# A Block whose closing barrier leaves out the drain of GpSimd

## The chip, the cores and the metric

The kernel runs on one core of a Trainium2 chip. The metric is the device time of one execution in microseconds (us).

Three stretches of the end of an execution are used throughout, all read from the trace:

- **A**: from the landing of the last output DMA to the end of the Block's last semaphore instruction. That instruction also ends the profile's span, except in one experiment, which is marked.
- **B**: from there to the last semaphore event of the record. It lies outside the span. In the trace of the kernel before it has nine counts of semaphore 2 between 829.68 and 830.27 us, then events of 196 semaphores, then nine counts again between 831.05 and 831.41 us. No recorded instruction of the program names semaphore 2. This document and the recorded texts call each group of nine counts a barrier of the runtime; the name is the author's reading.
- **G**: the pause between the two semaphore instructions with which GpSimd closes the Block (the first collects the arrivals of the other engines, the second lets them go).

A + B is the whole serial tail after the last byte of output has landed.

## The reference

A transformer block: layernorm with a modulation, linear attention, layernorm with a modulation, and a gated feed-forward part.

```python
def reference(A_x, A_wqkv, A_wo, B_x, B_w_gate, B_w_up, B_w_down, c, w_mod):
    ...                                   # A_x: 1 x 2048 x 1024, bf16
    mod = (_silu(c) @ w_mod).reshape(c.shape[0], 6, 1, -1)
    ...
    h = _layernorm(x, axis=-1) * (1 + ca) + sa
    x = x + ga * _A_ref(h, A_wqkv, A_wo)              # linear attention, 32 heads
    h = _layernorm(x, axis=-1) * (1 + cb) + sb
    x = x + gb * _B_ref(h, B_w_gate, B_w_up, B_w_down)  # silu(h @ gate) * (h @ up) @ down
    return x
```

The change does not touch the arithmetic.

## The kernel before

The kernel records a list of operations for each engine, works out the semaphore waits between them, and emits one program per engine into a Block. When the Block closes, all engines meet in a barrier. The parts that matter here are the Block, GpSimd's own work (57 small operations, no DMA), and the end of SyncE's program, which waits for every output DMA.

```python
    with ExitStack() as es:
        block = es.enter_context(nc.Block())
        ...
        P.pool("memset", ap=IDENT[:], constant=1.0)            # GpSimd's program begins
        P.pool("affine_select", out=IDENT[:], in_=IDENT[:], ...)
        P.pool("memset", ap=NEGHALF[:], constant=-0.5)
        ...
        def th2_mod():                                         # and ends with the fourth of these
            for dt in range(NDT):
                P.pool("tensor_scalar", out=H2T[:, dt, :], in0=H2T[:, dt, :], scalar1=MODCOL[:, 2, dt:dt + 1],
                       scalar2=MODCOL[:, 3, dt:dt + 1], op0=ALU.mult, op1=ALU.add)
        ...
                        out_ops.append(P.dma("out", ov[:, st, nh * 512 + c0:nh * 512 + c1], xs))   # from SyncE
        P.wait_for("sp", out_ops)
        ...
        engines = {"pe": block.tensor, "act": block.scalar, "dve": block.vector, "pool": block.gpsimd,
                   "sp": block.sync}
        P.emit(sems, engines)
```

As built, the Block of the kernel before closes in this way. TensorE, VectorE, ScalarE and SyncE each execute a DRAIN that also counts up a semaphore (96), and then wait for another one (97). GpSimd executes a plain DRAIN, waits until semaphore 96 stands at four, and raises semaphore 97 by four.

## Time and profile before

| | |
|---|---|
| time, median of the first 3 runs | 831.32 us (831.20 to 831.43) |
| span of the profiled run | 829.4 us |
| TensorE (PE) busy | 824.0 us, 99% |
| GpSimd (POOL) busy | 39.8 us, 5% |
| A, B, G | 0.771, 1.970, 0.414 us |

The first lines of the page of the kernel before give the span and each engine's busy time.

```profile
span 829.4 us, 10017 instructions
...
PE 824.0 (99%) x4083; PEld 378.4 (46%) x4083; DVE 312.0 (38%) x665; ACT 197.6 (24%) x336; POOL 39.8 (5%) x57
...
```

The chain of waits of the kernel before, in order of time (start us, us, what):

```profile
...
1.71 4.21 DMA xres<-in_A_x_dram
...
8.76 818.08 PE ps L176 x4069
826.83 0.02 issue
826.86 0.29 DVE xres L176
```

Between 8.76 and 826.84 us the chain is TensorE alone. As long as another engine does not keep TensorE waiting, it can only cost time before or after that stretch.

The next view has the instructions of the Block's own line (286) in the kernel before: engine, operation, count, then shortest, median and longest duration in ns, then the start of the first and of the last in us. The letter q marks the engine's sequencer.

```profile
...
L286 POOLq EVENT_SEMAPHORE  x2: 17/17/17, 828.9 to 829.3; - x2
L286 POOLq DRAIN  x1: 6939/6939/6939, 642.8 to 642.8; - x1
...
L286 SPq COMPARE_BRANCH  x1: 41/41/41, 828.7 to 828.7; - x1
L286 SPq DRAIN  x1: 13/13/13, 828.9 to 828.9; - x1
L286 SPq EVENT_SEMAPHORE  x1: 17/17/17, 829.4 to 829.4; - x1
...
```

GpSimd's DRAIN is the longest record of the group (6939 ns), but it starts at 642.8 us, 186 us before the barrier. A duration in such a list says nothing about cost until the start has been read. The two semaphore instructions of GpSimd start 0.4 us apart, at 828.9 and 829.3. The DMA queues of the kernel before (packets, MB, share):

```profile
...
q1 hardware_dynamic: 199184, 118.65, 52.7%
q8 instruction: 32, 0.52, 0.3%
q14 instruction: 13, 0.11, 0.0%
q10 hardware_dynamic: 16, 0.00, 0.0%
...
```

There is no queue of a software kind: GpSimd issues nothing.

The same tail with exact times, listed from the trace's instruction records (us from the start of the span; duration in ns):

```
last matmul ends            826.817
SyncE   last output issued  827.174
        last landing        828.668
SyncE   branch              828.684   41
SyncE   DRAIN (arrives)     828.865   13
GpSimd  semaphore 96 >= 4   828.903   17
GpSimd  semaphore 97 += 4   829.334   17     <- 0.414 us after the one before it ended
others  semaphore 97 >= 1   829.376 (first start) to 829.439 (last end)
        last event          831.409
```

In this trace the record of GpSimd's first semaphore instruction starts only when its semaphore is satisfied: the fourth arrival is counted at 828.879 us, and the record starts 0.024 us later, though GpSimd's instruction before it, the DRAIN, had ended at 649.773 us. The second one, which raises semaphore 97, has no semaphore to wait for at all, so the 0.41 us between them are not a wait for an engine that these records show.

### The profile page before, as it was taken

To read this page: it belongs to the slowest core of one execution; us is meant where nothing else is said; L and a number is where in the kernel's file an instruction comes from. 1 tells how busy PE (TensorE), PEld (TensorE's weight loads), DVE (VectorE), ACT (ScalarE), POOL (GpSimd) and SP (SyncE) were. 2 spreads that over 40 slices of the span, in tenths; PEclk is the share of its full clock that TensorE was granted. 3 is DMA by queue.
4 is the path that set the end of the run, shared out by engine and by line. 5 is a ranking of instruction groups with operands and counts; after the bars stand their busy time and mean duration, and the time that the engine had idled before them with its cause. 6 is when DMAs were issued, how large, how long until landed. Compare 5 with 4: busy or idle time off the path is not lost.

```text
span 829.4 us, 10017 instructions
## 1 busy us (share of the span) xinstructions
PE 824.0 (99%) x4083; PEld 378.4 (46%) x4083; DVE 312.0 (38%) x665; ACT 197.6 (24%) x336; POOL 39.8 (5%) x57
## 2 busy tenths in 40 slices
PE   8999999999999999999999999999999999999998
PEld 4544444454444444444444444444444444444444
DVE  5797986756955521121221111122111111221111
ACT  4757641323242111011111101111110111111011
POOL 1010000000130000030000003000000300000000
PEclk9999999999999999999999999999999999999999
DMA  9969655928397996700455570045557004553000
GB/s 320 288 151 229 149 159 172 202 102 304 60 258 225 259 267 174 192 25 14 128 150 155 150 188 28 15 126 153 153 153 187 26 18 125 154 151 86 0 26 26
DMA packets 199245, 119.28 MB, mean 144 GB/s; under 512 B 57880, under 2 KB 182944, under 8 KB 199200
## 3 DMA queue, kind: packets, MB, share of 16 engines
q1 hardware_dynamic: 199184, 118.65, 52.7%
q8 instruction: 32, 0.52, 0.3%
q14 instruction: 13, 0.11, 0.0%
q10 hardware_dynamic: 16, 0.00, 0.0%
HBM read 100.67 MB, written 4.33 MB: 127 GB/s over the span
## 4 chain that ended last, share of the span: by engine, by line
PE 99%; DMA 1%; DVE 0%; ACT 0%; SPq 0%; issue 0%
PE ps L176 99%; DMA xres<-in_A_x_dram 1%; DVE stats L176 0%; ACT xres L176 0%; SPq L176 0%; DVE xres L176 0%; DVE mv L176 0%; DVE nmr L176 0%
## 5 line engine op out<-in xcount | busy, mean ns | idle before, releaser
L176 PE MATMUL ps<-h2t,gug 128*128 128x512 bf16 x896 | 211.7, 379 | 0.0
L176 PE MATMUL ps<-h2t,guu 128*128 128x512 bf16 x896 | 211.7, 379 | 0.0
L176 DVE TENSOR_TENSOR at<-sg,ps 128x512 bf16<-128x512 bf16 x112 | 77.1, 688 | 282.7 <-PE ps L176 281.1
L176 ACT ACTIVATE sg<-ps 128x512 bf16<-128x512 f32 x112 | 66.9, 597 | 309.7 <-PE ps L176 309.7
L176 PEld LDWEIGHTS ps<-h2t,guu 128*128 128x128 bf16 x896 | 87.5, 98 | 105.8
L176 PEld LDWEIGHTS ps<-h2t,gug 128*128 128x128 bf16 x896 | 87.4, 98 | 105.7
L176 PE MATMUL ps<-wd_a,at 128*128 128x512 bf16 (+1 forms) x512 | 112.4, 378 | 0.0
L176 PE MATMUL ps<-ht,wqk 128*128 128x512 bf16 x512 | 111.7, 379 | 0.0
L176 PE MATMUL ps<-wd_b,at 128*128 128x512 bf16 (+1 forms) x384 | 85.0, 378 | 0.0
L176 PEld LDWEIGHTS ps<-wd_a,at 128*128 128x128 bf16 x512 | 50.0, 98 | 59.8
L176 DVE TENSOR_TENSOR ut<-att,gb_b 128x512 bf16<-128x512 bf16 (+1 forms) x32 | 13.8, 430 | 167.5 <-ACT att L176 167.5
L176 PEld LDWEIGHTS ps<-ht,wqk 128*128 128x128 bf16 x512 | 49.4, 98 | 58.8
L176 ACT ACTIVATE att<-ps 128x512 bf16<-128x512 f32 (+1 forms) x32 | 17.4, 591 | 182.1 <-PE ps L176 182.1
L176 PEld LDWEIGHTS ps<-wd_b,at 128*128 128x128 bf16 x384 | 37.5, 98 | 44.7
L176 PE MATMUL ps<-pk,xres 128*128 128x512 bf16 x256 | 56.5, 379 | 0.0
L176 PE MATMUL ps<-mw,pqt 128*128 128x512 bf16 x256 | 56.3, 379 | 0.0
L176 POOL TENSOR_SCALAR h2t<-h2t,modcol 128x512 bf16<-128x512 bf16 x32 | 26.4, 841 | 383.0 <-DMA h2t<-xn 383.0
L176 ACT ACTIVATE e<-ps 128x512 bf16<-128x512 f32 x56 | 33.1, 603 | 31.7 <-PE ps L176 20.5
L176 PEld LDWEIGHTS ps<-mw,pqt 128*128 128x128 bf16 x256 | 24.8, 98 | 30.3 <-DVE xres L176 0.4
L176 PEld LDWEIGHTS ps<-pk,xres 128*128 128x128 bf16 x256 | 24.8, 98 | 30.0 <-issue 0.4
L176 ACT ACTIVATE junk<-xres 128x1024 bf16<-128x1024 bf16 x24 | 25.4, 1058 | 35.1 <-DVE xres L176 34.9
L176 DVE SCALAR_TENSOR_TENSOR xres<-ps,xres 128x512 bf16<-128x512 f32 x32 | 21.4, 689 | 12.3 <-PE ps L176 11.7
(107 smaller groups left out, 346.0 us busy)
## 6 DMA issues: line engine op xcount, KB each, us to landing
gug<-in_B_w_gate_dram SPq DMA_DIRECT2D x56, 512.0 KB, 3.9
guu<-in_B_w_up_dram SPq DMA_DIRECT2D x56, 512.0 KB, 5.2
xres<-in_A_x_dram SPq DMA_DIRECT2D x20, 256.0 KB, 7.8
rb<-recip_den SPq DMA_DIRECT2D x8, 512.0 KB, 11.5
stgx<-in_w_mod_dram SPq DMA_DIRECT2D x2, 2048.0 KB, 7.8
wd_a<-in_B_w_down_dram SPq DMA_DIRECT2D x4, 1024.0 KB, 7.8
out_dram<-xres SPq DMA_DIRECT2D x31, 128.0 KB, 1.7
xres<-in_A_x_dram SPq DMA_DIRECT2D x3, 1024.0 KB, 14.0
```

Source lines behind the costliest of these rows:

```text
L176: return getattr(e, method)(**kw)
```

## The change

The intent is to end the Block without the drain of GpSimd, as GpSimd has no DMA in this kernel. The other engines are still to drain, and all engines to meet in a barrier of semaphores alone.

```diff
     with ExitStack() as es:
-        block = es.enter_context(nc.Block())
+        block = es.enter_context(nc.Block(no_gpsimd_drain=True))
```

As built, this removes GpSimd's DRAIN and gives each of the other four engines one semaphore instruction more: their DRAIN no longer counts up semaphore 96, a separate instruction behind it does.

## The prediction

> What bounds the kernel now. TensorE does: the page's first part gives PE 824.0 us busy of a span of 829.4 us (99%), and the chain of waits is PE from 8.76 us to 826.84 us almost without a break. The granted clock is 1.000. Only the first 8.8 us and the tail after the last matmul are not TensorE.
>
> The tail, read from the instructions of the Block's own line (line 286) and from the semaphore events: the last matmul ends at 826.84, VectorE adds until 827.15, SyncE issues the last output DMA at 827.17, it has landed at 828.67, and only then SyncE leaves its program (828.68) and runs its DRAIN (828.87, 13 ns). GpSimd sees the fourth arrival at 828.90, and releases everybody at 829.33; the others see it at 829.38 to 829.45. So the whole barrier after the last landing takes about 0.75 us, 0.09% of the time.
>
> What the change removes. One DRAIN of GpSimd. In the trace this DRAIN starts at 642.83 and lasts 6.94 us, ending at 649.77; it is long because it stands behind eight operations on GpSimd, the last of which ends at 649.71. It is over 178 us before the last output lands, so it is not on the critical path. Nor is there anything in a ring for it to wait for: no instruction of GpSimd issues a DMA. [...] all data packets (199,184 + 16) are of kind hardware_dynamic, issued by SyncE and ScalarE.
>
> What it adds. By the description of the flag the other four engines still drain, and then pass a barrier of semaphores alone. That may add one semaphore instruction on each engine; these last 17 to 51 ns each here. On SyncE, the last to arrive, this would be on the critical path: I estimate +0.03 to +0.1 us from those durations and from the 24 ns between SyncE's arrival and GpSimd's start.
>
> What it may move. Between GpSimd's two semaphore instructions lie 0.41 us at the end, but 0.06 us in the same pair at the program's start (0.583 to 0.600, then 0.661). I can't tell from this trace why. If the new barrier is built of other instructions, some of this 0.41 us may go. That is the most there is to gain: 0.41/831, 0.05%.
>
> Sum: between -0.4 and +0.15 us. The three runs before spread by 0.23 us, so the change should hardly be seen. Nothing in the engine programs themselves changes.
>
> Predicted time: 831.2 us, range 830.6 to 831.8. Chances: faster by over 2%: 0.004; within 2%: 0.992; slower by over 2%: 0.004.
>
> What would show each step right: in the profile after, GpSimd's DRAIN of the Block's line is gone (or no longer a plain DRAIN), its last multiplications still end near 650 us, PE's busy time stays within 1 us of 824.0, the last output DMA still lands about 1.5 us after issue, and the stretch from that landing to the last semaphore instruction is 0.3 to 0.9 us. Wrong: a changed PE busy time, a lower clock, or a tail longer than 1 us.
>
> What would make it wrong: a barrier of semaphores whose hops are serial through all five engines and dear; a runtime epilogue outside the span (the time exceeds the span by 1.8 us) which depends on that drain, so that its cost shows up there; or chips that differ by more than the 0.03% that the three runs show.

## The result

The kernel after took 831.42 us (median of 6 runs, 830.86 to 831.73), the kernel before 831.22 us (median of 6, 830.89 to 831.43). The ratio of fast runs is 1.0002, with a 95% interval of 0.9989 to 1.0015: the same. Ratios in this document are the mean time of one kernel's fast runs over that of the other's of the same rounds, so not quite the ratio of the medians quoted.

The page of the kernel after begins:

```profile
span 828.6 us, 10020 instructions
...
PE 823.5 (99%) x4083; PEld 379.1 (46%) x4083; DVE 312.6 (38%) x665; ACT 197.7 (24%) x336; POOL 39.9 (5%) x57
...
```

Its chain of waits:

```profile
...
1.69 3.68 DMA xres<-in_A_x_dram
...
8.21 818.07 PE ps L176 x4069
...
826.31 0.29 DVE xres L176
```

The span is 0.8 us shorter than before, and the change did not cause most of that. The matmul stretch is as long as before (818.07 against 818.08 us) but starts 0.55 us earlier, because the first input load on the chain took 3.68 us in place of 4.21. The change has not touched that load, and it varies from run to run: an experiment below has 4.47 us. A single pair of spans would have misled here.

The instructions of the Block's line in the kernel after:

```profile
...
L286 DVEq EVENT_SEMAPHORE  x2: 21/21/21, 826.7 to 828.6; - x2
L286 SPq EVENT_SEMAPHORE  x2: 17/17/17, 828.4 to 828.6; - x2
L286 POOLq EVENT_SEMAPHORE  x2: 17/17/17, 828.4 to 828.5; - x2
...
L286 SPq COMPARE_BRANCH  x1: 41/41/41, 828.1 to 828.1; - x1
L286 SPq DRAIN  x1: 7/7/7, 828.3 to 828.3; - x1
...
```

GpSimd's DRAIN is gone, SyncE has two semaphore instructions in place of one, and the two of GpSimd now start 0.1 us apart. With exact times, from the trace:

```
                        before     after
last landing           828.668   828.133
A                        0.771     0.496
G                        0.414     0.065
B                        1.970     2.414
A + B                    2.741     2.910
```

So the pause of 0.41 us did go out of the Block's barrier, and A became 0.275 us shorter. But B, outside the span, became 0.444 us longer. The runtime's own barrier shows where: each arrival counts up one semaphore (2), and between the second and the third count there lie 0.267 us before and 0.688 us after. In the runtime's last barrier before the program, and in the second of the two behind it, 0.038 us lie there, in both kernels. The sum moved by +0.17 us.

The times say the same about B without any trace of it: the device time less the span is 2.16 to 2.26 us in the six runs after, and 1.74 to 1.84 us in nine later runs of the kernel before. The two ranges are far apart, although the times themselves overlap.

### The profile page after: what moved, and what is told of

Same layout as the page of the kernel before. It is cut to its first block, busy times and chain, and to the rows that moved or that the text cites. A ratio compares the mean times of both kernels' runs of the same rounds, so it can differ in the third digit from the quotient of the medians.

```text
span 828.6 us, 10020 instructions
## 1 busy us (share of the span) xinstructions
PE 823.5 (99%) x4083; PEld 379.1 (46%) x4083; DVE 312.6 (38%) x665; ACT 197.7 (24%) x336; POOL 39.9 (5%) x57
## 4 chain that ended last, share of the span: by engine, by line
PE 99%; DMA 0%; DVE 0%; ACT 0%; SPq 0%; issue 0%
PE ps L176 99%; DMA xres<-in_A_x_dram 0%; DVE stats L176 0%; ACT xres L176 0%; SPq L176 0%; DVE xres L176 0%; DVE mv L176 0%; DVE nmr L176 0%
```

## The experiments

Two theories are tested.

- **Theory S (slot)**: the 0.41 us belongs to a fixed place in GpSimd's instruction stream. Removing the DRAIN moved every later instruction one place forward, so the pause fell on the next one, behind the program, where B lies. The cause supposed, that the next block of instructions is asked for at this place, is an estimate from a packet of 8,192 bytes on an instruction queue that starts at 830.06 us in the kernel before; no record shows it.
- **Theory D (drain)**: the pause is an after-effect of GpSimd's DRAIN, and the longer B is the runtime making up for a drain that was left out.

The results of the runs about the place of the pause, from their profiles (the four runs with late work or with a DMA on GpSimd follow in their own sections). A, B and G come from one profile of each label. The last column, the device time less the span, covers all timed runs of the label (for the kernel before, its 23 runs beside the experiments), and so shows for every run whether B was long. The experiments ran in three sets, each on another chip; a time is compared only with the kernel before of its own set. Drain means the DRAIN that the Block itself emits, except in the run named after_drain. The column "count" gives GpSimd's recorded instructions against the 69 of the kernel before; the removed drain is a minus one in it.

```
label            drain  count   G      A      B     A+B   time - span
before           yes      0    0.414  0.771  1.970  2.741   1.74-1.84
ctl_before       yes      0    0.414  0.771  1.972  2.743   1.76-1.82
after            no      -1    0.065  0.496  2.414  2.910   2.16-2.26
ctl_after        no      -1    0.066  0.494  2.384  2.878   2.16-2.20
before_plus1     yes     +1    0.068  0.419  1.918  2.337   1.70-1.76
before_minus1    yes     -2    0.060  0.415  2.258  2.673   2.04-2.11
after_plus1      no       0    0.423  0.861  1.962  2.823   1.78-1.79
after_plus2      no      +1    0.073  0.511  1.910  2.421   1.68-1.77
after_drain      own      0    0.418  0.856  1.968  2.824   1.81-1.83
before_plus128   yes   +128    0.375  0.732  1.964  2.696   1.75-1.81
```

### Controls

The two kernels were run again with nothing but a comment added.

> A control: the kernel before, with a comment added. Call A the stretch from the last output's landing to the end of the Block's last semaphore instruction, B the stretch from there to the last semaphore event of the record [...], and G the pause between GpSimd's two semaphore instructions of the Block. The first profile of this kernel had A 0.77, B 1.97, G 0.41 us. Both theories expect the same again within 0.05 us, and a ratio of 1.000 within 0.001.

> A control: the kernel after, with a comment added. Its first profile had A 0.50, B 2.41, G 0.065 us: what the Block's barrier gained in A came back in B. Both theories expect the same again within 0.05 us, and a ratio between 0.9995 and 1.0008. If B falls to 1.97, the giving back was an accident of one profile.

Measured: 831.26 us (ctl_before) and 831.36 us (ctl_after), beside 831.45 us for the kernel before; both ratios are 0.9998 (0.9984 to 1.0011, and 0.9986 to 1.0011). A, B and G repeat within 0.03 us. So the tail is much steadier than the time: the runs of the kernel before in the second set below lie between 830.62 and 832.18 us, but in these two pairs of profiles the tail repeats to some hundredths. A question of 0.1 us has to be put to the tail.

### One GpSimd instruction more, with the drain

```diff
         P.pool("memset", ap=NEGHALF[:], constant=-0.5)
+        P.pool("memset", ap=NEGHALF[:], constant=-0.5)
```

> The kernel before, with its drain, and one more GpSimd memset at the start (the same constant written twice). Theory S (slot): the pause of 0.41 us belongs to a fixed place in GpSimd's instruction stream; one instruction more puts that place at or before the wait for the four arrivals, where it hides: G 0.065, A about 0.42, B about 1.97, so A+B about 2.39 against 2.74. Theory D (drain): the pause is an after-effect of GpSimd's plain drain: G 0.41, A 0.77, B 1.97 as in the kernel before.

Measured: G 0.068, A 0.419, B 1.918, and a time of 830.75 us against 831.45 us (ratio 0.9992, 0.998 to 1.0005). This is the expectation of theory S (G and A as expected, B 0.05 us shorter). Theory D falls here: the drain is where it was, as the Block's line shows, and the pause behind it is gone.

```profile
...
L286 POOLq EVENT_SEMAPHORE  x2: 17/17/17, 828.8 to 828.9; - x2
L286 POOLq DRAIN  x1: 6951/6951/6951, 642.8 to 642.8; - x1
...
```

The DMA view shows where the pause went. First the kernel before in the last microseconds, from 820 to 832 us (packets, MB, share). Queue q14 seems to bring instructions to the engines other than TensorE. This is an estimate from counts: the 13 packets of q14 (8,192 bytes each) hold 59.8 bytes for each of the 1,781 instructions that the trace records for these engines, and the 32 of q8 (16,384 bytes each) hold 63.7 for each of TensorE's 8,236, two figures near each other; the run with 128 more gives 64 below.

```profile
...
q1 hardware_dynamic: 432, 0.26, 7.0%
q14 instruction: 1, 0.01, 0.3%
...
```

The kernel before has no packet of q14 between 645 and 655 us. The kernel with one memset more, from 645 to 655 us:

```profile
...
q8 instruction: 1, 0.02, 0.6%
q14 instruction: 1, 0.01, 0.3%
...
```

Its view from 820 to 832 us has a line for q1 alone. So one packet of 8,192 bytes on the instruction queue, which started at 830.06 us, now starts at 650.84 us, when GpSimd had finished its last operations (its DRAIN, from 642.8 us, lasted 6.951 us) and had nothing to do. With it the pause went out of the tail, which is 2.337 us in place of 2.741. In the kernel before the packet itself starts 1.1 us after the pause begins (828.92 and 830.06 us), so the pause is not the wait for those bytes to arrive; that the pause is the sequencer's work of asking for them is the author's reading, and no record shows it.

### One GpSimd instruction fewer, with the drain

```diff
-        P.pool("memset", ap=NEGHALF[:], constant=-0.5)
+        P.dve("memset", ap=NEGHALF[:], constant=-0.5)
```

> The kernel before, with its drain, and one GpSimd instruction fewer (the memset of one constant is given to VectorE). Theory S: the pause moves one instruction later, out of the Block and into the runtime's barrier, as in the kernel after, although the drain is still there: G 0.065, A about 0.42, B about 2.39. Theory D: G 0.41, A 0.77, B 1.97.

Measured: G 0.060, A 0.415, B 2.258, 831.40 us (ratio 0.9998, 0.9985 to 1.0012). The pause moved out of the Block into the runtime's barrier, with the drain still in place, as theory S has it.

But the edit did more than was meant. The trace has two GpSimd instructions fewer, not one: 67 against 69. With the constant made by VectorE, the semaphore instruction ahead of GpSimd's first `rstd` operation is gone too, as that operation no longer has two semaphores to wait for. So, by the count, the pause lies one place later than in the kernel after, whose 68 instructions end right before it. This fits the last packet of q14: it starts 1.57 us after the Block's last GpSimd instruction has ended, against 1.13 and 1.10 us in the kernel after and its control. B is 0.13 us smaller than expected: in this run the pause costs 0.34 us over the run with one memset more (2.673 against 2.337), while in the kernel after it costs 0.46 us over its own counterpart (2.878 against 2.421). That the other place is the reason is likely, but not shown.

### One and two GpSimd instructions more, without the drain

The same edit as in the run with one memset more, once and twice, on the kernel after.

> The kernel after (no drain of GpSimd) with one memset more at GpSimd's start, so that GpSimd has as many instructions ahead of its last semaphore instruction as in the kernel before. A, B, G as defined for the control of before. Theory S (a fixed slot in the instruction stream[...]): the pause returns to the place that it had with the drain: G 0.41, A about 0.84, B about 1.97, though there is no drain. Theory D (the drain causes the pause, and the runtime makes up for a missing one): G 0.065, A 0.50, B 2.39.

> The kernel after with two memsets more. Theory S: the pause hides before the wait, the last 8 KB record of the instruction queue moves from about 830 us to about 650 us, G 0.065, A 0.50, B about 1.93; A+B about 2.43, or 0.09 more than the kernel before with one memset more (2.34), because the barrier of semaphores alone has one more step on SyncE. Theory D: A 0.50, B 2.39.

Measured with one more: G 0.423, A 0.861, B 1.962. Here GpSimd has no drain, and the pause of 0.42 us is back at its old place, because as many instructions stand ahead of it as before. Measured with two more: G 0.073, A 0.511, B 1.910, A + B 2.421. B is back at its short length (1.970 in the kernel before) although there is no drain, so nothing in B makes up for one. The times, 831.83 (2 runs) and 831.41 us (4 runs) beside 831.13 us for the kernel before, decide nothing, and nor do those of the next two experiments (831.52 and 831.13 us, 2 runs each).

One detail of the expectation failed: with two more, the moved record of 8 KB appears at 356.67 us, not near 650 us. The author's estimate is that without a DRAIN nothing holds GpSimd's sequencer until its engine has finished, so that it runs ahead of work that has not begun. That this explains the 356 us is not shown; that the sequencer can be ahead of its engine is shown by the late operations below, where its last semaphore instruction, at 829.3 us, comes before the last operation starts, at 829.842.

### The drain alone given back

```diff
-        block = es.enter_context(nc.Block())
+        block = es.enter_context(nc.Block(no_gpsimd_drain=True))
         ...
+        P.add("pool", lambda e: e.drain(), tag="drain")
         P.wait_for("sp", out_ops)
```

> The flag is kept, and a plain drain is put at the end of GpSimd's own program: the removed instruction alone is given back. It runs at 643 to 650 us, behind the last eight operations. If only its slot counts (theory S): the same as one memset more: G 0.41, A about 0.84, B about 1.97. Theory D expects the same, with G 0.41; so this run tells only whether the drain costs more than a memset: it should not, A+B within 0.05 us of the run with one memset more.

Measured: G 0.418, A 0.856, B 1.968, A + B 2.824 (with a memset in its place 2.823). In this place a drain and a memset cost the same within 0.001 us. Against the kernel before (2.741), which differs only in the kind of barrier, the barrier of semaphores alone costs 0.08 us; the two runs with the pause hidden differ by as much (2.421 against 2.337). Most of it is the one step more on SyncE: from the start of its DRAIN to GpSimd's first semaphore instruction it is 0.038 us in the kernel before, and 0.109 us in the kernel after.

### 128 GpSimd instructions more

```diff
+        for _ in range(128):
+            P.pool("memset", ap=NEGHALF[:], constant=-0.5)
         P.wait_for("sp", out_ops)
```

> The kernel before with 128 memsets more at the end of GpSimd's program, where it is idle (about 13 us, ending near 663 us). 8192 bytes are 128 instructions if one takes 64 bytes. Theory S with that period: one 8 KB record more in the instruction queue, and the pause comes back at the same place as in the kernel before: G 0.41, A 0.77, B 1.97, last 8 KB record near 830 us. If the place is not periodic, or has another period: G 0.065, A 0.42 and B 1.92 as with one memset more.

The 64 bytes of the expectation agree with the counts of the kernel before: 63.7 bytes for each recorded instruction of TensorE in the packets of q8.

Measured: G 0.375, A 0.732, B 1.964; one 8 KB record more than the kernel before (at 500.19 us), and the last one at 829.81 us. (The memsets took 20 us and not 13, which changes nothing here.) So the place comes back after 128 instructions, with one packet of 8,192 bytes more, or 64 bytes for each. Counted in the order of the program, the pause lies behind the 68th recorded instruction of GpSimd wherever it shows in the Block of a run without these 128, and here behind the 196th. In the kernel before all packets of q14 within the program have 8,192 bytes, and the 32 of q8 have 16,384. The period fits a pause once per packet of 8,192 bytes, and in the serial tail it costs 0.41 us on GpSimd. That the packet is what causes it was not shown, nor was it measured what a packet costs elsewhere in the program.

### Late work on GpSimd, with and without the drain

Here the drain is given something to wait for. The output stays correct, as the buffer written is not read again.

```diff
+        for dt in range(4):
+            P.pool("tensor_scalar", out=H2T[:, dt, :], in0=XRES[:, NST - 1, 512:1024], scalar1=MODCOL[:, 2, dt:dt + 1],
+                   scalar2=MODCOL[:, 3, dt:dt + 1], op0=ALU.mult, op1=ALU.add)
         P.wait_for("sp", out_ops)
```

> The drain is given something to wait for. Kernel before, with four more GpSimd operations at the end (each some 0.77 us, on the last output tile, into a buffer that nobody reads; the output is unchanged). They start at about 827.2 and end near 830.3, after the last landing at about 828.7. The drain must hold GpSimd's arrival: A about 1.8 (against 0.42 to 0.77), B about 1.95. Ratio about 1.0015.

> The same four late operations, with the flag of the change: no drain of GpSimd. The Block's barrier should then pass while GpSimd still works: A about 0.5. Theory R (the runtime's own barrier after the Block waits for the engine anyway): B grows to about 3.3, and A+B is the same as with the drain within 0.2 us. Theory N (nobody waits): B 1.9 to 2.0, A+B about 2.4, that is 1.3 us less than with the drain.

With the drain: the late operations on GpSimd's timeline (start us, us, what), then the Block's line:

```profile
...
827.13 3.01 POOL L176 TENSOR_SCALAR h2t<-xres,modcol 128x512 bf16<-128x512 bf16 x4 [177.63 <-DVE xres L176]
```

```profile
...
L286 POOLq EVENT_SEMAPHORE  x2: 17/17/17, 830.2 to 830.3; - x2
...
L286 POOLq DRAIN  x1: 2657/2657/2657, 827.5 to 827.5; - x1
...
L286 SPq DRAIN  x1: 7/7/7, 828.6 to 828.6; - x1
...
```

SyncE arrives at 828.6 us, but GpSimd's DRAIN lasts until its last operation has ended (830.142 us; the DRAIN ends at 830.197), and the barrier follows at 830.2. A is 1.978 (about 1.8 was expected) and B 1.910 us. Without the drain:

```profile
...
827.60 3.02 POOL L176 TENSOR_SCALAR h2t<-xres,modcol 128x512 bf16<-128x512 bf16 x4 [177.55 <-DVE xres L176]
```

```profile
...
L286 SPq EVENT_SEMAPHORE  x2: 17/17/17, 829.2 to 829.3; - x2
L286 POOLq EVENT_SEMAPHORE  x2: 17/17/17, 829.2 to 829.3; - x2
...
```

GpSimd passes the barrier at 829.2 and 829.3 us, in the middle of its work: its third late operation runs from 829.093 to 829.860, and the fourth starts only at 829.842. So a barrier without a drain does not say that GpSimd has finished. A is 0.495 us to the last semaphore instruction (the span itself ends later here, with the last operation), and from there B is 3.14 us. The runtime's barrier waits: between its second and third count there are 1.445 us. This is theory R of the expectation, apart from a small saving. The comparison that fits this pair is from the end of the last GpSimd operation to the last event: 2.19 us with the drain, 1.94 us without, so 0.25 us saved, in one profile of each (the expectation allowed 0.2). Little of it is the drain's own time: the DRAIN ended 0.055 us after the work, and the Block's barrier took another 0.226 us, from 830.197 to 830.423 us. Without the drain this barrier runs beside the work. The times fit, 832.38 and 831.96 us (4 runs each), but the intervals of their ratios to the kernel before overlap (0.9997 to 1.0027, and 0.9991 to 1.0021).

The chain of waits of the run without the drain has a first load of 4.47 us, where the kernel before had 4.21 and the kernel after 3.68. That is the scatter of the start that was spoken of above:

```profile
...
1.70 4.47 DMA xres<-in_A_x_dram
...
9.01 818.07 PE ps L176 x4069
...
```

### A DMA from GpSimd, with and without the drain

The last of the 33 output transfers is issued by GpSimd. SyncE waits for it as for the others.

```diff
-                        out_ops.append(P.dma("out", ov[:, st, nh * 512 + c0:nh * 512 + c1], xs))
+                        out_ops.append(P.dma("outp" if c0 > 0 else "out", ov[:, st, nh * 512 + c0:nh * 512 + c1], xs,
+                                             queue="pool" if c0 > 0 else "sp"))
```

> The ring is given something. Kernel before, with the last of the 33 output transfers (32 KB) issued by GpSimd instead of SyncE; SyncE still waits for all of them. The drain now has a ring that was used. If a drain of a used ring is dear: A over 1.0. If it only waits for the landing: A 0.42 to 0.85 as before[...]. Ratio 1.000 to 1.002.

> The same with the flag of the change: no drain of the used ring. A about 0.5 unless the slot of the pause falls between GpSimd's two semaphore instructions (then 0.85). If the drain of a used ring was dear, A+B is shorter than with the drain by that cost; if not, the two differ only by the pause's place and by the 0.09 us of the extra step, under 0.2 us without the pause.

The ring was really used. The queues of the run with the drain (packets, MB, share) now have one of a software kind:

```profile
...
q0 software_dynamic: 32, 0.03, 0.0%
...
```

The Block's line of the same run:

```profile
...
L286 POOLq EVENT_SEMAPHORE  x2: 17/17/17, 830.0 to 830.1; - x2
...
L286 POOLq DRAIN  x1: 2026/2026/2026, 827.6 to 827.6; - x1
...
L286 SPq DRAIN  x1: 13/13/13, 829.8 to 829.8; - x1
...
```

Now the DRAIN seems really to wait for a transfer: it starts at 827.600 and ends at 829.626 us, 0.08 us after the landing at 829.544, while GpSimd's own DMA instruction had ended at 828.38. So in this profile a used ring is not dear to drain; the drain ends just after the landing. (The transfer itself was slower: it landed 1.92 us after its issue began, against 1.49 us from SyncE in the kernel before.) What delays the barrier is again the pause, behind the 68th instruction as before, which is the DRAIN here: GpSimd's first semaphore instruction starts at 830.032, 0.41 us after the drain ended, while SyncE had arrived at 829.81. So some 0.2 us of the pause are left to pay. A is 0.677 and A + B 2.615 us. Without the drain the pause falls between the two semaphore instructions (G 0.414), A is 0.896 and A + B 2.893 us. So here the flag makes the tail 0.28 us longer, through the place of the pause and the extra step. No pair with the pause put at the same place was run for this form. The times are 831.69 and 832.02 us (4 runs each), beside 831.40 us: no difference is clear of noise.

### A version that beats both

The kernel before with one GpSimd memset more has the shortest tail of all: 2.337 us, against 2.74 for the kernel before and 2.88 to 2.91 for the kernel after. In time this is 0.05%, and its interval (0.998 to 1.0005) does not prove it. It is also no gain to keep: a later edit that changes the number of GpSimd's instructions can move the place again, as one more and two fewer did here.

## Why the prediction was right or wrong

The prediction, 831.2 us in a range of 830.6 to 831.8, was right: 831.42 us. The time is a weak test of it: what the change could move by the prediction's own sum (-0.4 to +0.15 us) is smaller than that range, so a wrong account of the tail would have come out right too. What tests the steps is the tail in the trace.

- *TensorE bounds the kernel, and GpSimd's DRAIN is not on the critical path.* Right. The matmul stretch is 818.07 us against 818.08, and the removed 6.94 us were worth nothing. Where the work before the drain is memsets, as in the run with 128 more, the same DRAIN lasts 168 ns.
- *Nothing in a ring to wait for.* Right for this kernel: its page has no queue of a software kind. The run with a DMA from GpSimd suggests that it would not have been much either: its drain ended 0.08 us after the landing.
- *One semaphore instruction more on SyncE costs 0.03 to 0.1 us.* Right: 0.07 us on that step, 0.08 us over the whole tail at an equal place of the pause.
- *Some of the 0.41 us between GpSimd's two semaphore instructions may go; the cause can't be told.* The pause went from there, all of it (0.065 us are left), but nothing was gained. The step that fails is its accounting: it counted the 0.41 us as a thing of the barrier, which would be gone with the barrier's form. It is a thing of the place in the instruction stream (it moves with one instruction and comes back after 128), and it fell on the runtime's barrier behind the span, where B grew by 0.44 us.
- *A tail of 0.3 to 0.9 us after the landing.* Right, 0.496 us; but this measure ends with the span, and so it does not see B.
- *A runtime epilogue outside the span that depends on the drain* was named as what could make it wrong. The epilogue did grow, by 0.4 us, but the drain is not the reason: without a drain and with two memsets more, B is 1.910 us.

The sum for the kernel after is thus +0.14 to +0.17 us, at the edge of the predicted -0.4 to +0.15. It cannot be told in the time, in which single runs of the kernel before spread by up to 1.7 us within one set.

## What to carry to other kernels

The length of a drain's record is not its price: the 6.94 us here were worth nothing, as they ended 179 us before the barrier. Ask when it ends, and who arrives last at the barrier. A saving that shows in the span may be returned behind it (here 0.275 us in A against 0.444 us in B), so compare the device time less the span as well, before believing a few tenths of a microsecond. Of the cases tried here, leaving out GpSimd's drain shortened the tail (by 0.25 us, not clear in the time) only where GpSimd was the last engine to finish, and then the Block's end no longer said that its work was done.

What was measured here for such a comparison: the pause took 0.38 to 0.42 us between GpSimd's two semaphore instructions, and 0.34 to 0.49 us of the tail where it fell on the runtime's barrier. Device time less span was 1.7 to 1.8 us without the pause there, and 2.0 to 2.3 us with it. GpSimd's drain ended 0.066 us after its last operation in the kernel before, 0.055 us in the run with late work and the drain.
